# Two feed-forward networks behind attention: a second network's first products are threaded into a states' block, and late splits, stores and loads move by a few places

## The chip, the cores and the metric

The kernel runs on one core of a Trainium2 chip. The metric is the device time of one execution in microseconds; the time of a version is the median of its runs. TensorE (PE) does the matrix products, VectorE (DVE), ScalarE (ACT) and GpSimd (POOL) the work on their results, and SyncE (SP) issues nearly all DMAs of the stretch that is discussed here.

## The reference

Attention between 512 tokens and 32 states for 8 batches and 8 heads, then a gated network on all 8 x 544 rows of 512 columns, then a second network on the result:

```python
x = concatenate([softmax(x st') st, softmax(st x') x])   # per batch and head, D = 64
x = x.transpose(0, 2, 1, 3).reshape(B * S, H * D)         # 4352 rows, 512 columns
g = x @ w_gate                                            # 512 x 1536
x = (silu(g) * (x @ w_val)) @ w_out                       # first network
h = x @ w_in                                              # 512 x 2048
out = (maximum(h, 0) + alpha * minimum(h, 0)) @ w_out2    # second network
```

All is fp32. The kernel gets this precision from split operands: a number is the sum of a high part (`hi`, a copy rounded by ACT) and a low part (`lo`, the difference, made by DVE in `sub_lo`, L83), and a product is three matrix passes, high x high, high x low and low x high (`PASSES`). In the profile, ACT's line 77 is a copy (a high part or a move out of PSUM), and DVE's line 83 a low part.

## The kernel before

The work runs in stages. Attention and the first network of the 8 batches of 512 tokens come first, interleaved. Then comes the first network for the 256 state rows, the **states' block**: an object of class `Block` with n = 256 columns. Then the second network.

**The states' block.** `ffn1` goes through f = 0 to 11, the 128-wide blocks of the hidden layer: `gate(f)` (12 matmuls into bank g, then ACT's silu), `value(f)` (12 into bank v, then DVE's product, L488), `split(f)` (ACT's high and DVE's low part), and `project(f - 1)` (12 into four accumulators acc0 to acc3). Between these calls `fill(f, i)` runs what the table `slots` holds for the place: `split_w` (splitting later weights: ACT, then DVE), `x2_pair(0)` (the inputs of the second network's first pair of batches: loads, differences, high and low parts), `ahead` (weight loads). `finish` adds the last projection, copies the accumulators out and stores them (L512).

**The second network** takes the batches in pairs. A pair with a block of the hidden layer of 2 x 128 rows is a **step**, t = 0 to 31; steps 32 to 39 (`LAST` = 32, `hidden_last`) do the states. A step forms its 2 x 2 blocks of hidden values in 7 products, not 8, and has 7 **places**. Place by place `hidden_pair` makes one product of 6 matmuls (banks g, v, aux, v, g, v, aux) and what follows it on the other engines, and then `fill()` pops one item of the list `work`: half of a **link**, that is, one of the 14 half-steps (`link`, `project`, 6 matmuls, L1006) that put the hidden values of the two steps before through the output weights. A link's result is added to a running sum by DVE (L1017), or, the first time, copied by ACT (L77, sum<-acc). So in t = 2 to 31 TensorE alternates between a product and a link half.

The hidden values of a step are h00, h10, h11, h01 (`raised`: the leaky step, three ACT instructions L872 to L874 and one POOL addition L875); POOL then makes the four differences T1, T3, T2, T4 in this order (`less`, L915). All have to be split into high and low parts before the links use them; these splits fall into the next step, as the entries of the dictionary `left`, and `late(key)` runs them at written places: T1 at place 3, T3 at place 4, T2 and T4 at place 5.

**Other traffic.** `load_wo` (L993) loads a link's weights, three links ahead; at the end of an odd step the first three are loaded together, six DMAs. `load_w2` (L759) loads product weights. `give` (L1041 to L1044) turns a finished sum around with a DVE transpose and stores it with four DMAs, at every third place. `x2_sums` (L791, L792) makes differences of the next pair's inputs on DVE and stores them for a later load; `give_last` and `turn` do the last pair's output by transposes on TensorE.

**Order.** TensorE runs in written order throughout. In the loop over t = 0 to 31, DVE, ACT and POOL run in written order too (`manual_schedule`); SP, and all engines' work but TensorE's in the states' block and in t = 32 to 39, are put in order by the framework's scheduler. Every engine runs its own queue strictly in order: an instruction that waits holds all behind it.

Of the kernel before, what the change touches and what calls it, by code (L numbers as in the profile page):

```python
# [25 lines left out]
def attention_and_two_ffns(ctx: ExitStack, tc: tile.TileContext, x, state, w_gate, w_val,  # L26
                           w_out1, w_in2, w_out2, alpha, out):
    nc = tc.nc
# [430 lines left out]
    class Block:  # L459


        def __init__(self, n, lhs, rhs, nk, keep=False):
            self.n, self.lhs, self.rhs, self.nk, self.keep = n, lhs, rhs, nk, keep
            self.acc, self.p, self.hid = None, {}, {}

# [11 lines left out]
        def gate(self, f):  # L477

            if self.keep:
                if f % 2 == 0:  # L480
                    self.kept = t4([P, 2, S], F32, "p")
                self.p[f] = self.kept[:, f % 2]
            else:
                self.p[f] = t2([P, S], F32, "s")[:, :self.n]
            return nc.scalar.activation(self.p[f], self.product(f, 0, "g"), AF.Silu)

        def value(self, f):
            return nc.vector.tensor_tensor(out=self.p[f], in0=self.p[f], in1=self.product(f, 1, "v"),  # L488
                                           op=ALU.mult)
# [24 lines left out]
    def ffn1(blk, slots, before):  # L514
# [19 lines left out]
    with tc.manual_schedule(engines={mybir.EngineType.PE}):  # L534
# [248 lines left out]
        def x2_sums(pr):  # L783
# [108 lines left out]

        def hidden_pair(t, fill):
# [30 lines left out]
            def late(key):  # L924
                left.pop(key, lambda: None)()

# [5 lines left out]
            fill()  # L932
            v = psum([P, S], "v")
# [3 lines left out]
            fill()  # L937
            late("t1")
            y = aux([P, S])
            product(y, 2)  # L940
            fill()
            late("t3")
            product(v, 3, start=False)
# [8 lines left out]
            fill()  # L952
            product(v, 5, start=False)
# [4 lines left out]
            fill()  # L958
            product(y, 6, start=False)
# [3 lines left out]
            fill()  # L963
            lo("h00", h00)
# [10 lines left out]
            for k, o in (("t1", h00), ("t3", h01), ("t2", h11), ("t4", h10)):  # L975
                left[k] = lambda k=k, o=o: (hi(k, o), lo(k, o))

        acc, sums, put_in, giving, turning = {}, {}, set(), [], []
# [45 lines left out]
        def give(pr, to, e):  # L1024
# [17 lines left out]
            for i in range(4):  # L1042
                dst = out[c * T:c * T + S, d * P + 32 * i:d * P + 32 * i + 32]
                nc.sync.dma_start(dst.rearrange("(t r) n -> r t n", r=32), o[32 * i:32 * i + 32])  # L1044

        def give_last(pr, to, e):
# [6 lines left out]
            def turn():  # L1053
# [5 lines left out]
                nc.sync.dma_start(out[c * T:c * T + S, d * P:(d + 1) * P].rearrange("(k p) n -> p k n", k=SC), o)  # L1059
# [18 lines left out]
        def hidden_last(t, fill):  # L1078
            pr, s = STEPS[t]
            x, w = x2[pr], ws2.pop(t)  # L1080
            for f in range(2):
# [9 lines left out]
                h = hid["s", 2 * s + f] = t4([P, 2, S], F32R, "h2")  # L1091
                acopy(h[:, 0, :NS], m)
                sub_lo(h[:, 1, :NS], m, h[:, 0, :NS])
                fill()

# [7 lines left out]
        slots = {}  # L1103
        for f in range(2, NF1):
            slots.setdefault((f - 2, 0), []).append(lambda f=f: split_w(f))
        early = x2_pair(0)
        for i, th in enumerate(early):
            slots.setdefault((1 + i * (NF1 - 2) // len(early), 2), []).append(th)
        slots.setdefault((NF1 - 2, 2), []).append(lambda: [ahead() for _ in range(3)])

        def lhs(f, k, a, which):
            return ws[f][:, k, a, which, :]

        blk = Block(NS, lhs, lambda k, c: xs[0][:, k, c], NPAIR)
        ffn1(blk, slots, lambda: blocks[B - 1].finish(B - 1))
        blk.finish(B)

        LAST = (B // 2) * NJ2
        def step(t, pr, s):
            for n in ((t + 1,) if t == LAST - 1 else (t + 1, t + 2) if t == LAST else (t + 2,) if t > LAST else ()):  # L1120
                if n < len(STEPS):
                    load_last(n)
# [7 lines left out]
            def fill():  # L1130
                places[0] += 1
                for _ in range(len(turning)):
                    turning.pop(0)()
# [11 lines left out]
            (hidden_pair if t < LAST else hidden_last)(t, fill)  # L1145
# [11 lines left out]

        forming, work = {}, [lambda: None for _ in range(2 * 7 + 1)]
# [5 lines left out]
        for t in range(LAST, len(STEPS)):  # L1164
            step(t, *STEPS[t])
        for th in turning + work:
            th()
# [30 lines left out]
```

## Time and profile before

| what | value |
|---|---|
| time before, median of 3 runs | 1483.83 us (1479.69 to 1485.51) |
| profiled execution, its own time | 1478.91 us |
| span of the profiled execution, first to last instruction | 1477.1 us |
| mean granted TensorE clock | 0.981 of full speed |
| busy: PE | 1379.3 us, 93% |
| busy: DVE, ACT, POOL | 1033.7 us (70%), 822.6 us (56%), 558.8 us (38%) |

The table is read from the top: the runs give the time; the profile is one execution, and its own time is what durations read from the trace add up to. TensorE's busy share includes time at a lower granted clock, in which a matmul takes longer.

### The profile page before, as it was taken

To read this page: it belongs to the slowest core of one execution; us is meant where nothing else is said; L and a number is where in the kernel's file an instruction comes from. 1 tells how busy PE (TensorE), PEld (TensorE's weight loads), DVE (VectorE), ACT (ScalarE), POOL (GpSimd) and SP (SyncE) were. 2 spreads that over 40 slices of the span, in tenths; PEclk is the share of its full clock that TensorE was granted. 3 is DMA by queue.
4 is the path that set the end of the run, shared out by engine and by line. 5 is a ranking of instruction groups with operands and counts; after the bars stand their busy time and mean duration, and the time that the engine had idled before them with its cause. 6 is when DMAs were issued, how large, how long until landed. Compare 5 with 4: busy or idle time off the path is not lost.

```text
span 1477.1 us, 20530 instructions
## 1 busy us (share of the span) xinstructions
PE 1379.3 (93%) x7192; PEld 1067.1 (72%) x7192; DVE 1033.7 (70%) x1591; ACT 822.6 (56%) x1408; POOL 558.8 (38%) x422
## 2 busy tenths in 40 slices
PE   5799999999898999999989999999989999999897
PEld 2467776767676776778967777778777777778686
DVE  6778536678697877443756878778886788778740
ACT  6656344555655645333557566755656567655532
POOL 4432112233142322000046566545664565555611
PEclk7999999999999999999999999999999999999999
DMA  9442250676959575202264786779756987676772
GB/s 265 169 151 50 72 137 9 184 222 186 253 170 274 145 217 137 73 1 73 79 235 150 253 274 202 188 225 314 240 153 178 314 294 230 170 241 205 285 254 91
DMA packets 274224, 271.92 MB, mean 184 GB/s; under 512 B 133704, under 2 KB 198216, under 8 KB 273096
## 3 DMA queue, kind: packets, MB, share of 16 engines
q1 hardware_dynamic: 271976, 270.21, 59.1%
q8 instruction: 57, 0.93, 0.3%
q10 hardware_dynamic: 2144, 0.39, 0.2%
q14 instruction: 47, 0.39, 0.1%
HBM read 206.05 MB, written 64.49 MB: 183 GB/s over the span
## 4 chain that ended last, share of the span: by engine, by line
PE 57%; DVE 16%; ACT 10%; issue 6%; DMA 5%; POOL 4%; SPq 2%; POOLq 0%; ACTq 0%; DVEq 0%
PE acc L503 16%; PE v L472 9%; PE g L472 9%; PE acc L1006 8%; DVE h L83 6%; PE v L903 3%; PE aux L442 3%; DVE u L911 3%; PE g L903 2%; PE aux L903 2%; DMA wo<-ws2d 2%; ACT h L77 2%; DVE sum L1017 2%; ACT m L874 2%; DMA raw<-in_moe_w_out_dram 2%
## 5 line engine op out<-in xcount | busy, mean ns | idle before, releaser
L1006 PE MATMUL acc<-h,wo 128*128 128x512 f32 x1344 | 349.4, 396 | 36.5 <-DVE sum L1017 19.0
L1006 PEld LDWEIGHTS acc<-h,wo 128*128 128x128 f32 x1344 | 251.5, 190 | 101.2 <-DVE sum L1017 28.1
L503 PE MATMUL acc<-h,wp 128*128 128x512 f32 (+1 forms) x1296 | 297.1, 380 | 7.1 <-DVE h L83 3.7
L503 PEld LDWEIGHTS acc<-h,wp 128*128 128x128 f32 x1296 | 234.3, 189 | 57.7 <-DVE h L83 4.9
L875 POOL TENSOR_TENSOR u<-u,m 128x512 f32<-128x512 f32 x96 | 128.5, 1338 | 354.3 <-ACT m L874 322.7
L83 DVE TENSOR_TENSOR h<-u,h 128x512 fp32r<-128x512 f32 x160 | 159.0, 1009 | 69.4 <-ACT h L77 68.4
L472 PE MATMUL g<-a,sw 128*128 128x512 f32 x576 | 155.9, 405 | 9.7 <-ACT sw L77 5.4
L472 PEld LDWEIGHTS g<-a,sw 128*128 128x128 f32 x576 | 105.1, 190 | 71.3 <-issue 26.0
L472 PE MATMUL v<-a,sw 128*128 128x512 f32 x576 | 154.8, 405 | 0.1
L903 PE MATMUL v<-x,w 128*128 128x512 f32 x576 | 148.7, 394 | 5.0 <-DVE u L911 5.0
L872 ACT ACTIVATE m<-u 128x512 f32<-128x512 f32 x96 | 60.3, 628 | 157.8 <-DVE u L911 153.1
L1017 DVE TENSOR_TENSOR sum<-acc,sum 128x512 f32<-128x512 f32 x184 | 125.2, 681 | 27.2 <-PE acc L1006 26.9
L472 PEld LDWEIGHTS v<-a,sw 128*128 128x128 f32 x576 | 107.7, 192 | 33.8 <-issue 9.8
L903 PEld LDWEIGHTS v<-x,w 128*128 128x128 f32 x576 | 109.0, 190 | 30.0 <-DVE u L911 7.1
L83 DVE TENSOR_TENSOR h<-h,h 128x512 fp32r<-128x512 f32 (+1 forms) x80 | 77.7, 972 | 62.5 <-ACT h L77 62.0
L284 POOL TENSOR_TENSOR m<-m,raw 128x512 int32<-128x512 int32 x44 | 61.1, 1393 | 154.1 <-DVE m L276 75.2
L77 ACT ACTIVATE h<-u 128x512 fp32r<-128x512 f32 x160 | 96.6, 622 | 28.3 <-POOL u L915 28.3
L488 DVE TENSOR_TENSOR s<-s,v 128x512 f32<-128x512 f32 (+1 forms) x84 | 54.2, 645 | 81.8 <-PE v L472 68.3
L915 POOL TENSOR_TENSOR u<-u,u 128x512 f32<-128x512 f32 x64 | 103.1, 1611 | 5.0
L83 DVE TENSOR_TENSOR sw<-aux,sw 128x512 fp32r<-128x512 f32 x96 | 62.7, 683 | 56.3 <-ACT sw L77 56.3
L903 PE MATMUL aux<-x,w 128*128 128x512 f32 x384 | 101.1, 400 | 0.0
L77 ACT ACTIVATE h<-s 128x512 fp32r<-128x512 f32 (+1 forms) x84 | 50.3, 598 | 89.9 <-DVE s L488 89.7
(148 smaller groups left out, 2145.8 us busy)
## 6 DMA issues: line engine op xcount, KB each, us to landing
wo<-ws2d SPq DMA_DIRECT2D x224, 256.0 KB, 4.8
w<-w2d SPq DMA_DIRECT2D x104, 512.0 KB, 5.5
w2d<-sp SPq DMA_DIRECT2D x32, 512.0 KB, 4.0
raw<-in_moe_w_out_dram SPq DMA_DIRECT2D x14, 1024.0 KB, 5.0
x2r<-x2d SPq DMA_DIRECT2D x25, 512.0 KB, 5.8
w<-w2d SPq DMA_DIRECT2D x48, 256.0 KB, 5.1
x2d<-xo SPq DMA_DIRECT2D x32, 256.0 KB, 3.5
raw<-in_moe_w_in_dram SPq DMA_DIRECT2D x8, 1024.0 KB, 6.2
```

The lines of the kernel that those rows point to most:

```text
L77: return nc.scalar.activation(o, i, AF.Copy)
L83: (eng or nc.vector).tensor_tensor(out=o, in0=src, in1=hi.bitcast(F32), op=ALU.subtract)
L284: nc.gpsimd.tensor_tensor(out=m, in0=m, in1=lo, op=ALU.add)
L472: nc.tensor.matmul(o[:, :self.n], self.lhs(f, k, a, which), self.rhs(k, c), start=(i == 0), stop=(i == last))
L488: return nc.vector.tensor_tensor(out=self.p[f], in0=self.p[f], in1=self.product(f, 1, "v"), op=ALU.mult)
L503: nc.tensor.matmul(self.acc[e][:, :self.n], wo1[f // 2][:, f % 2, a, e * P:(e + 1) * P], t[:, c, :self.n], start=(f == 0 and i == 0), stop ...
L872: nc.scalar.activation(n, src, AF.Relu, scale=-1.0)
L875: nc.gpsimd.tensor_tensor(out=out, in0=out, in1=n, op=ALU.add)
L903: nc.tensor.matmul(o, w[:, a, q], x[k][:, q, e], start=start and n == 0, stop=stop and n == 5, skip_group_check=True)
L915: nc.gpsimd.tensor_tensor(out=o, in0=x0, in1=x1, op=ALU.subtract)
L1006: nc.tensor.matmul(o, w[:, f, a, e], h[:, q], start=first and i == 0, stop=i == 5, skip_group_check=True)
L1017: nc.vector.tensor_tensor(out=r, in0=o, in1=r, op=ALU.add)
```

## The change

Four things, in the order of the program:

1. **The states' block.** Its `split(f - 1)` is called behind `gate(f)` and not `split(f)` behind `value(f)`. Its four accumulators share two PSUM banks, as halves of acc0 and acc1; since two groups of matmuls then accumulate in one bank, both banks are set to zero by DVE (two 128x512 MEMSETs) ahead of `project(0)` and no matmul carries the start flag. From f = 7 on (`FROM`) the block's gate and value products go to acc2 and acc3, which frees g and v, and two products of steps t = 0 and 1 are called per f (10 of the 14 ahead of `finish`, 4 behind it). `x2_pair` is packed into f = 1 to 6, two items per f; before, it was spread over f = 1 to 10. To be called in parts, `hidden_pair` yields behind each place.
2. **T2 and T4.** Their high parts (ACT) are called at place 4, ahead of `raised(h11)`; their low parts (DVE) stay at place 5.
3. **Stores.** The four DMAs of `give` are issued two places later, the store of `x2_sums` three, that of `turn` one (the list `sending`).
4. **Order and the end.** SP is in written order now, and so are all engines in the states' block and in t = 32 to 39. In t = 32 and 33 the splits that step 31 left are run at places (`LATE`); before, all were run ahead of t = 32. The splits of `hidden_last` run one place later (`soon`), and `load_last` is called a little later.

```diff
@@ class Block
         def project(self, f):
             if f == 0:
-                self.acc = [psum([P, S], f"acc{e}") for e in range(NPAIR)]
+                if self.n == S:
+                    self.acc = [psum([P, S], f"acc{e}") for e in range(NPAIR)]
+                else:
+                    pairs = [psum([P, 2, self.n], f"acc{e}") for e in range(NPAIR // 2)]
+                    for t in pairs:
+                        nc.vector.memset(t, 0.0)
+                    self.acc = [pairs[e // 2][:, e % 2] for e in range(NPAIR)]
...
-                                     t[:, c, :self.n], start=(f == 0 and i == 0),
-                                     stop=(f == NF1 - 1 and i == 2))
+                                     t[:, c, :self.n], start=(self.n == S and f == 0 and i == 0),
+                                     stop=(f == NF1 - 1 and i == 2), skip_group_check=self.n < S)
...
             blk.gate(f)
+            if f and blk.n < S:
+                blk.split(f - 1)
             fill(f, 0)
             blk.value(f)
-            blk.split(f)
+            if blk.n == S:
+                blk.split(f)
@@ def x2_sums
-                nc.sync.dma_start(xt2d[pr - 1][:, k], r[to])
+                sending.append([3, lambda: nc.sync.dma_start(xt2d[pr - 1][:, k], r[to])])
@@ def hidden_pair
             late("t3")
+            late("t2 hi")
+            late("t4 hi")
             product(v, 3, start=False)
...
             fill()
-            late("t2")
-            late("t4")
+            yield
+            late("t2 lo")
+            late("t4 lo")
             product(g, 4, start=False)
@@ def give
-            for i in range(4):
...
-                nc.sync.dma_start(dst.rearrange("(t r) n -> r t n", r=32), o[32 * i:32 * i + 32])
+            def send():
...
+            sending.append([2, send])
@@ def step
+        LATE = {(0, 1): ("h10 hi", "h10 lo"), (0, 2): ("t1",), (1, 1): ("t3", "t2 hi", "t4 hi"),
+                (1, 2): ("t2 lo", "t4 lo")}
...
             def fill():
                 places[0] += 1
+                for e in list(sending):
+                    e[0] -= 1
+                    if not e[0]:
+                        sending.remove(e)
+                        e[1]()
...
+                for key in LATE.get((t - LAST, places[0]), ()):
+                    late(key)
+                for th in soon:
+                    th()
+                soon.clear()
@@ the states' block and the loop
-        with tc.manual_schedule(engines={mybir.EngineType.DVE, mybir.EngineType.Activation, mybir.EngineType.Pool}):
-            for t in range(LAST):
-                step(t, *STEPS[t])
-            for th in left.values():
-                th()
+        with tc.manual_schedule(engines={E.DVE, E.Activation, E.Pool, E.SP}):
...
+            for i, th in enumerate(x2_pair(0)):
+                slots.setdefault((1 + i // 2, 2), []).append(th)
+            slots.setdefault((4, 2), []).append(lambda: [ahead() for _ in range(3)])
+            first = (_ for t in range(2) for _ in step(t, *STEPS[t]))
+            for i in range(2 * (NF1 - FROM)):
+                slots.setdefault((FROM + i // 2, 0 if i % 2 == 0 else 2), []).append(lambda: next(first))
...
+            blk.banks = lambda f: ("g", "v") if f < FROM else ("acc2", "acc3")
+            ffn1(blk, slots, lambda: blocks[B - 1].finish(B - 1))
+            blk.split(NF1 - 1)
+            blk.finish(B)
+            for _ in first:
+                pass
```

How this moves instructions is shown at three places. First VectorE at the start of the states' block. The rows are those of f = 0 to 2: L488 (L489 in the changed file) is the product with bank v, `h` a low part of the block's hidden values, `ws` a low part of split weights. Before:

```order
L83 TENSOR_TENSOR h_1155_6319<-s_1151_6287,h_1155_6319 128x256
L80 COPY xo_1158_6340<-acc2_1086_5863 128x512
L488 TENSOR_TENSOR s_1160_6346<-s_1160_6346,v_1163_6364 128x256
L83 TENSOR_TENSOR h_1164_6378<-s_1160_6346,h_1164_6378 128x256
L488 TENSOR_TENSOR s_1174_6407<-s_1174_6407,v_1177_6425 128x256
```

and of the change:

```order
L83 TENSOR_TENSOR h_1161_6360<-s_1151_6289,h_1161_6360 128x256
L83 TENSOR_TENSOR ws_1162_6363<-wr_63_344,ws_1162_6363 128x4x256
L489 TENSOR_TENSOR s_1159_6345<-s_1159_6345,v_1163_6366 128x256
L505 MEMSET acc0_1164_6380 128x512
L505 MEMSET acc1_1165_6381 128x512
L848 TENSOR_TENSOR x2t_1170_6404<-x2r_1167_6398,x2r_1166_6396 128x1024
```

The two MEMSETs stand behind the low part of some weights and behind the second product with bank v. Next ScalarE at places 4 and 5 of step t = 5. `h<-u` and `h<-h` on L77 are high parts, L872 to L874 (L882 to L884 in the changed file) the leaky step of h11 and then of h00. Before:

```order
L77 ACTIVATE h2_1364_7606<-h_1360_7583 128x512
L77 ACTIVATE h2_1382_7717<-u_1369_7633 128x512
L872 ACTIVATE m_1385_7730<-u_1384_7728 128x512
L873 ACTIVATE u_1384_7728<-u_1384_7728 128x512
L874 ACTIVATE m_1385_7730<-m_1385_7730,alpha_sb_82 128x512
L77 ACTIVATE h2_1382_7717<-u_1356_7552 128x512
L77 ACTIVATE h2_1388_7747<-u_1363_7604 128x512
L872 ACTIVATE m_1391_7759<-g_1373_7651 128x512
```

and of the change:

```order
L77 ACTIVATE h2_1362_7605<-h_1358_7582 128x512
L77 ACTIVATE h2_1380_7715<-u_1367_7632 128x512
L77 ACTIVATE h2_1380_7715<-u_1354_7554 128x512
L77 ACTIVATE h2_1381_7719<-u_1361_7603 128x512
L882 ACTIVATE m_1384_7731<-u_1383_7729 128x512
L883 ACTIVATE u_1383_7729<-u_1383_7729 128x512
L884 ACTIVATE m_1384_7731<-m_1384_7731,alpha_sb_82 128x512
L882 ACTIVATE m_1389_7758<-g_1371_7651 128x512
```

The last two high parts of the differences, T2 and T4, stand ahead of the three instructions for h11 now. Last SP around the six loads at the end of step t = 11, the first weights of a new pair of steps' links (`wo2`). `out` x4 is a store of `give`, `w2` product weights, `x2r` inputs of a later pair. Before:

```order
L1044 DMA out_0_dram<-o_1587_8856 32x16x32 x4
L759 DMA w2_1589_8873<-w2d4_104 128x1024
L759 DMA w2_1595_8917<-w2d4_104 128x1024
L1044 DMA out_0_dram<-o_1601_8938 32x16x32 x4
L993 DMA wo2_1602_8945<-ws2d2_110 128x512
L993 DMA wo2_1602_8945<-ws2d3_111 128x512
L993 DMA wo2_1603_8948<-ws2d2_110 128x512
L993 DMA wo2_1603_8948<-ws2d3_111 128x512
L993 DMA wo2_1604_8951<-ws2d2_110 128x512
L993 DMA wo2_1604_8951<-ws2d3_111 128x512
L759 DMA w2_1606_8961<-w2d4_104 128x512
L780 DMA x2r_1608_8973<-x2d4_91 128x1024
```

and of the change:

```order
L1068 DMA out_0_dram<-o_1586_8859 32x16x32 x4
L769 DMA w2_1593_8917<-w2d4_104 128x1024
L1015 DMA wo2_1600_8941<-ws2d2_110 128x512
L1015 DMA wo2_1600_8941<-ws2d3_111 128x512
L1015 DMA wo2_1601_8944<-ws2d2_110 128x512
L1015 DMA wo2_1601_8944<-ws2d3_111 128x512
L1015 DMA wo2_1602_8947<-ws2d2_110 128x512
L1015 DMA wo2_1602_8947<-ws2d3_111 128x512
L769 DMA w2_1604_8957<-w2d4_104 128x512
L790 DMA x2r_1606_8969<-x2d4_91 128x1024
L790 DMA x2r_1607_8971<-x2d5_92 128x1024
L1068 DMA out_0_dram<-o_1599_8938 32x16x32 x4
```

The store that stood just ahead of the six loads stands three rows behind them; the store of the sum before it stands one row ahead of them.

## Rows read from the trace of the kernel before

**Rows 1.** Busy time by stretch (us): PE, PEld, DVE, ACT, POOL; granted clock; DMA share.

```profile
742.30:775.10 32.80, 26.36 (x105) 19.92 (x104) 17.81 (x20) 20.67 (x37) 15.26 (x12) 0.95 0.74 264
775.10:1388.10 613.00, 582.05 (x2497) 470.43 (x2496) 487.00 (x604) 383.92 (x662) 353.19 (x239) 0.99 0.71 226
...
981.00:983.00 2.00, 2.00 (x6) 1.58 (x5) 0.99 (x2) 0.00 (x0) 1.48 (x2) 0.52 1.03 352
```

**Rows 2.** TensorE in order of time: start, duration, instruction [idle before <-releaser].

```profile
696.06 1.60 PE L503 MATMUL acc<-h,wp 128*128 128x256 f32 x12
...
775.10 1.54 PE L903 MATMUL aux<-x,w 128*128 128x512 f32 x6
...
801.04 1.52 PE L903 MATMUL g<-x,w 128*128 128x512 f32 x6
...
803.76 1.52 PE L903 MATMUL v<-x,w 128*128 128x512 f32 x6
...
847.10 1.66 PE L1006 MATMUL acc<-h,wo 128*128 128x512 f32 x6 [1.03 <-DVE sum L1017]
...
979.73 2.24 PE L1006 MATMUL acc<-h,wo 128*128 128x512 f32 x6 [2.72 <-DMA wo<-ws2d]
...
1388.11 1.11 PE L1087 MATMUL g<-x,w 128*128 128x256 f32 x8
...
1401.37 2.93 PE L1006 MATMUL acc<-h,wo 128*128 128x512 f32 x6 [6.10 <-DVE sum L1017]
```

**Rows 3.** What TensorE waited for, 775.1 to 1388.1: total us, times, longest.

```profile
PE acc L1006 <- DVE sum L1017: 12.9, 18, 1.7
PE acc L1006 <- DMA wo<-ws2d: 11.6, 5, 3.8
PE acc L1006 <- ACT sum L77: 4.7, 3, 2.7
PE v L903 <- DVE u L911: 1.5, 3, 0.5
```

**Rows 4.** VectorE in order of time, places 4 and 5 of step t = 5.

```profile
844.47 1.98 DVE L83 TENSOR_TENSOR h<-u,h 128x512 fp32r<-128x512 f32 x2 [1.90 <-ACT h L77]
846.37 0.68 DVE L1017 TENSOR_TENSOR sum<-acc,sum 128x512 f32<-128x512 f32 x1
```

**Rows 5.** ScalarE in order of time: states' block, step t = 5, step t = 10.

```profile
694.82 0.38 ACT L485 ACTIVATE s<-g 128x256 f32<-128x256 f32 x1 [0.83 <-PE g L472]
696.79 0.42 ACT L77 ACTIVATE h<-s 128x256 fp32r<-128x256 f32 x1 [1.58 <-DVE s L488]
...
842.01 0.63 ACT L872 ACTIVATE m<-u 128x512 f32<-128x512 f32 x1 [5.17 <-DVE u L911]
...
843.82 1.14 ACT L77 ACTIVATE h<-u 128x512 fp32r<-128x512 f32 x2
...
943.91 0.63 ACT L872 ACTIVATE m<-u 128x512 f32<-128x512 f32 x1 [3.01 <-DVE u L911]
```

**Rows 6.** GpSimd in order of time, the differences T4 of three steps.

```profile
837.95 2.15 POOL L915 TENSOR_TENSOR u<-u,u 128x512 f32<-128x512 f32 x1
...
942.02 1.63 POOL L915 TENSOR_TENSOR u<-u,u 128x512 f32<-128x512 f32 x1
...
1397.73 1.27 POOL L915 TENSOR_TENSOR u<-u,u 128x512 f32<-128x512 f32 x1
```

**Rows 7.** SP's DMA queue in order of time, end of step t = 11.

```profile
974.71 1.97 SPq L1044 DMA_DIRECT2D out_dram<-o  x4
976.78 2.83 SPq L993 DMA_DIRECT2D wo<-ws2d  x6
```

**Rows 8.** Groups by line: count, ns min/median/max, first and last start.

```profile
L83 DVE TENSOR_TENSOR ws<-wr,ws x9: 1217/1219/1227, 686.2 to 722.4; 128x1024 fp32r<-128x1024 f32 x9
L77 ACT ACTIVATE ws<-wr x8: 1042/1046/1061, 687.5 to 719.3; 128x1024 fp32r<-128x1024 f32 x8
...
L93 DVE MEMSET bd<- x2: 272/272/272, 0.9 to 1.2; 128x256 f32 x2
```

More of the change, by code (lines that the diff above doesn't have):

```diff
@@ L464, in __init__ @@
             self.acc, self.p, self.hid = None, {}, {}
+            self.banks = lambda f: ("g", "v")
         def product(self, f, which, tag):
@@ L484, in gate @@
                 self.p[f] = t2([P, S], F32, "s")[:, :self.n]
-            return nc.scalar.activation(self.p[f], self.product(f, 0, "g"), AF.Silu)
+            return nc.scalar.activation(self.p[f], self.product(f, 0, self.banks(f)[0]), AF.Silu)
         def value(self, f):
-            return nc.vector.tensor_tensor(out=self.p[f], in0=self.p[f], in1=self.product(f, 1, "v"),
+            return nc.vector.tensor_tensor(out=self.p[f], in0=self.p[f], in1=self.product(f, 1, self.banks(f)[1]),
                                            op=ALU.mult)
@@ L891, in attention_and_two_ffns, with late @@
         left = {}
+        def late(key):
+            left.pop(key, lambda: None)()
         def hidden_pair(t, fill):
@@ L974, in hidden_pair @@
             left["h10 lo"] = rest
-            for k, o in (("t1", h00), ("t3", h01), ("t2", h11), ("t4", h10)):
+            for k, o in (("t1", h00), ("t3", h01)):
                 left[k] = lambda k=k, o=o: (hi(k, o), lo(k, o))
-        acc, sums, put_in, giving, turning = {}, {}, set(), [], []
+            for k, o in (("t2", h11), ("t4", h10)):
+                left[k + " hi"] = lambda k=k, o=o: hi(k, o)
+                left[k + " lo"] = lambda k=k, o=o: lo(k, o)
+        acc, sums, put_in, giving, turning, sending, soon = {}, {}, set(), [], [], [], []
         def store(u, o):
@@ L1041, in give @@
             nc.vector.transpose(out=o.rearrange("p t n -> p (t n)"), in_=y)
-            for i in range(4):
-                dst = out[c * T:c * T + S, d * P + 32 * i:d * P + 32 * i + 32]
-                nc.sync.dma_start(dst.rearrange("(t r) n -> r t n", r=32), o[32 * i:32 * i + 32])
+            def send():
+                for i in range(4):
+                    dst = out[c * T:c * T + S, d * P + 32 * i:d * P + 32 * i + 32]
+                    nc.sync.dma_start(dst.rearrange("(t r) n -> r t n", r=32), o[32 * i:32 * i + 32])
+            sending.append([2, send])
         def give_last(pr, to, e):
@@ L1058, in turn @@
                 acopy(o, pt)
-                nc.sync.dma_start(out[c * T:c * T + S, d * P:(d + 1) * P].rearrange("(k p) n -> p k n", k=SC), o)
+                sending.append([1, lambda: nc.sync.dma_start(
+                    out[c * T:c * T + S, d * P:(d + 1) * P].rearrange("(k p) n -> p k n", k=SC), o)])
             turning.append(turn)
@@ L1101, in ahead @@
                 coming.pop(0)()
[L1103 to L1116, printed above, removed]
         LAST = (B // 2) * NJ2
+        LATE = {(0, 1): ("h10 hi", "h10 lo"), (0, 2): ("t1",), (1, 1): ("t3", "t2 hi", "t4 hi"),
+                (1, 2): ("t2 lo", "t4 lo")}
         def step(t, pr, s):
-            for n in ((t + 1,) if t == LAST - 1 else (t + 1, t + 2) if t == LAST else (t + 2,) if t > LAST else ()):
-                if n < len(STEPS):
-                    load_last(n)
+            if t == LAST:
+                load_last(t + 1)
             if s == 1 and pr + 1 < B // 2:
@@ L1131, in fill @@
                 places[0] += 1
+                for e in list(sending):
[3 more added lines that the diff above has]
+                        e[1]()
+                if t == LAST - 1 and places[0] == 4:
+                    load_last(LAST)
+                if t >= LAST and places[0] == 1 and t + 2 < len(STEPS):
+                    load_last(t + 2)
+                for key in LATE.get((t - LAST, places[0]), ()):
[3 more added lines that the diff above has]
+                soon.clear()
                 for _ in range(len(turning)):
@@ L1144, in step @@
                 x2_last()
-            (hidden_pair if t < LAST else hidden_last)(t, fill)
+            if t < LAST:
+                yield from hidden_pair(t, fill)
+            else:
+                hidden_last(t, fill)
             if t >= LAST:
```

35 lines of the change are left out of this document (27 added, 8 removed).

## The prediction

> **What bounds the kernel now.** I read busy time by stretch first, then TensorE in order of time. From step t = 2 to the end of step 31, 613 us, TensorE is busy 582.05 us and no other engine over 487.00 us [rows 1]: TensorE sets the pace, and its losses are what can be won. An undisturbed place is a product and a link half in 803.76 - 801.04 = 2.72 us [rows 2]. From the product at 775.10 to the first of step 32 at 1388.11 there are 5 places of step 2 and 7 in each of steps 3 to 31: 208 x 2.72 = 565.8 us of the 613.0. So **47.2 us are lost**. TensorE's waits in this stretch sum to 12.9 + 11.6 + 4.7 + 1.5 = 30.7 us [rows 3]. The rest is slow running after them: behind the 2.72 us wait at 979.73 the granted clock is 0.52 of full speed for two microseconds, that is, the lower of its two levels (1.2 GHz) for nearly all of that time [rows 1, 2]. A microsecond of wait thus costs 47.2 / 30.7 = 1.54 us. Two more losses lie outside. From 742.30 to 775.10 TensorE runs 17 groups of 6 matmuls (steps 0 and 1, and three groups of step 2), 17 x 1.36 = 23.1 us of work in 32.8: 9.7 lost [rows 1]. And it waits 6.10 us at 1401.37 in step 32 [rows 2].
>
> **Part 2, T2 and T4: the sums' waits.** At place 5 VectorE waits 1.90 us for ScalarE, makes two low parts in 1.98 us and only then the link's sum, at 846.37 [rows 4]; TensorE's next link half needs the bank that this sum empties and starts at 847.10, 1.03 us late [rows 2]. ScalarE makes these two high parts at 843.82, behind the three instructions for h11, for which it stood idle 5.17 us [rows 5]. GpSimd had T4 ready at 837.95 + 2.15 = 840.10 [rows 6]. With the high parts in front of h11's instructions they can run from 840.10 to 841.24, which is 0.77 us before those could start at 842.01. VectorE, idle from 844.47 - 1.90 = 842.57, then finds them done, and the next sum is some 1.90 us earlier: more than the 1.03 us of the wait. The edit adds no instruction. Its cover is that idle time, and it is thinner elsewhere: in step 10 T4 is ready at 943.65 and h11 starts at 943.91 [rows 6, 5], so one high part of 0.57 us makes h11 0.3 us late, on ScalarE, which has idle time behind it.
> All waits for sums, 12.9 + 4.7 = 17.6 us [rows 3], come within some 6 us behind such a pair of low parts. VectorE is busy 487 of 613 us, and will be 487 of about 577, 84%, so some will come back where several low parts and a difference of the next inputs fall on one place. I take three quarters, 13 us; ends: half, 9, and all, 17.6. The 1.5 us for u stay.
>
> **Part 3, the stores: the waits for weights.** SP waits until a transposed sum is ready, issues its four DMAs in 1.97 us from 974.71, and only then the six loads of the next links' weights, from 976.78 [rows 7]; TensorE's link has been waiting for them since 977.01 and starts at 979.73 [rows 2]. Now this store stands behind the six loads, and the one ahead of them is two places old, so its data are ready. The loads go at least the 1.97 us earlier, and SP's wait before it goes too. Five such waits make 11.6 us [rows 3]; five times 1.97 is 9.9. I take 10.6; ends: 8 (a store ahead still costs something) and 11.6.
> A rule of the Trainium skill speaks against this (DMA: Bandwidth & Descriptors, section "Issuing engines are not separate DMA queues"): all DMAs end up on the same 16 engines, and the time to issue one is usually small beside the transfer. By it the move would win little, and the sum below would lose its 10.6. Here the issue of one store alone is 1.97 us of a wait of 2.72 us, so I go by the row; the rule's outcome is a rival below.
> Parts 2 and 3 together: (13 + 10.6) x 1.54 = **-36.3 us**; ends (9 + 8) x 1.54 = -26.2 and (17.6 + 11.6) x 1.54 = -45.0.
>
> **Part 1, the states' block.** The gain: 10 of the 14 products of steps 0 and 1 stand between products of the block and so have their waits covered. At most the 9.7 us. The cost: until now the block has TensorE gapless. `project(0)` would be due at 696.06 [rows 2]. It now waits for a MEMSET of its bank, and that one stands on VectorE behind the second value product, behind a low part of weights, behind ScalarE's high part of them, behind the high part of the hidden values, behind the second silu. In durations: the silu ends at 694.82 + 0.38 = 695.20 [rows 5]; high part 0.42 [rows 5]; ws high 1.05 and ws low 1.22 [rows 8]; value product 0.42, taken as long as that high part of the same width; a MEMSET of 128x512, of which the trace has none: twice the 0.27 of a 128x256 one [rows 8] is 0.54, at least 0.27. Sum: 698.85, so TensorE waits **2.8 us**, and 1 to 1.8 more at the lower clock behind it, by the 1.54. When I lay out the changed order with such durations, four later f lose 0.2 to 0.4 us and f = 5 about 1.5, since `split(f - 1)` gives each low part less lead and `x2_pair`'s differences, packed into six f, stand ahead of it. That makes 6 to 7 us. The four products left behind `finish` and the first link halves keep about 3 us of the old waits. Net: -9.7 + 6.5 + 3 = **0**; ends -6 (VectorE and ScalarE in a better order than I lay out) and +7 (also the second half of the block stalls).
>
> **Part 4, the end.** At 1401.37 TensorE waits for sums that stand on VectorE behind the left-over splits, the last of which needs T4 from GpSimd at 1397.73 [rows 2, 6]. Spread over two steps, the sums no longer stand behind them. The splits of `hidden_last` one place later cost one short wait of about 1 us at the first half of a states' product, by laying the rows out. -6.1 + 1 and the slow clock behind: **-5.5**; ends -3 and -7. The last steps' chain is as before. `load_last` later and stores of the last pair one place later cost nothing as long as SP's loads come a whole step (some 5 us) ahead of their use.
>
> **Sum.** -36.3 + 0 - 5.5 = -42 on the profiled execution's 1478.9, so 1437. The runs before lie 0.8 to 6.6 us above that execution, their median 4.9; I add 4: **1441 us**. With all ends: 1478.9 + 4 - 45.0 - 6 - 7 = 1425, and 1478.9 + 4 - 26.2 + 7 - 3 = 1461.
>
> **Rivals.**
> - *VectorE takes the place of the wait.* The waits move to other sums, since VectorE at 84% has no room, and of part 2 only a quarter is won, 4 us: (4 + 10.6) x 1.54 + 5.5 = 28 won: about 1455; with nothing won, 1461. For it: low parts of 0.99 us x 2 stand ahead of every such sum still. Against: VectorE's idle 1.90 us lies before the pair, so the pair moves as a whole. The Trainium skill has a rule that points this way (Perfetto Trace Analysis, section "Optimization Strategy"): a bubble that repeats on the engine that should be full can mean too few buffers for the next tile, here accumulator banks, which the change doesn't add.
> - *The weights come late anyway*, because the transfers themselves are late: part 3 wins 2 us of 11.6. (13 + 2) x 1.54 + 5.5 = 28.6 won, about 1454. Against it: five waits alone, each behind a store.
> - *The states' block stalls through*: at f = 7 to 11 bank and low part come late each time, 2 us at each of 5 f and the lower clock, +15: 1456.
> - *Slower: GpSimd's T4 is late at place 4.* Then ScalarE's queue holds h11's three instructions behind the wait, and h11, h00 and all that follow are late in each step. The rows show 0.77 us and -0.3 us of room. To undo 42 us and 7 more over 30 steps it takes 1.6 us on TensorE in each. Against it: GpSimd is busy 353 of 613 us [rows 1] and starts these differences from the step before, and shorter waits of TensorE between there and place 4 are only the five for weights. The time then: 1490.
>
> **Chances.** My forecast 0.62; VectorE 0.11, weights 0.06, states' block 0.06 (all three faster still); all waits gone and the transition's too (1425 or less) 0.03; T4 late 0.12, of which 0.07 at the 1.2 to 1.6 us a step that cancel the gains and 0.05 beyond. The range 1425 to 1462 takes in the first four. Under 0.5%, 7.4 us, a measurement can't tell a change from none. Faster by more than that: 0.88; within: 0.07; slower: 0.05.
>
> **What would show it.** Right: TensorE's waits between step 2 and 32 down from 30.7 to about 8 us; none for wo over 1 us; no wait of VectorE for ScalarE ahead of the two low parts; a wait of about 3 us of `project(0)` for a MEMSET; a wait under 1.5 us in step 32. Wrong: ScalarE waiting for GpSimd ahead of h11's instructions (L882); SP's loads of wo waiting for a transposed sum; TensorE waiting for sums as long as before.

## The result, and the profile after

The changed kernel takes 1432.38 us (median of 4 runs, 1428.03 to 1433.43) against 1484.67 us for the kernel before (median of 4): ratio 0.9643, 95% interval 0.9604 to 0.9681. The forecast was 1441 us, with a range of 1425 to 1462. The profiled execution takes 1428.03 us, 50.9 us less than that of before.

Where the 50.9 us come from is read from three marks on TensorE: the first product of the states' block, the product of step 2 at place 3, and the first product of step 32. The start of the states' block alone lies between 686.8 and 694.5 us in the kernels below, whose work ahead of it is the same, so whole times hide small differences that the first two stretches show: kernels with the same instructions in them agree within 0.1 us from the block to step 2 (changed, stores back, splits flushed) and within 0.5 us in steps 2 to 31 (changed, old states' block, splits flushed and the three with early MEMSETs). The last stretch is less exact: with the same instructions it takes 83.7 or 85.3 us, and 1.5 us of that are its last twelve matmuls (3.41 us in the changed kernel, 4.87 with early MEMSETs). The kernels ran in several batches, in which the kernel before took 1482.3 to 1484.7 us; each ratio is taken within its batch.

| kernel | block to step 2 | steps 2 to 31 | step 32 to the end | median of all runs |
|---|---|---|---|---|
| before | 87.5 | 613.0 | 89.0 | 1484.7 |
| changed | 87.3 | 568.4 | 83.7 | 1432.4 |
| T2 and T4 alone | 86.7 | 581.1 | 89.5 | 1451.2 |
| stores alone | 87.5 | 600.4 | 91.6 | 1470.5 |
| changed, high parts back | 88.5 | 597.6 | 84.3 | 1465.3 |
| changed, stores back | 87.3 | 608.0 | 85.4 | 1471.3 |
| changed, old states' block | 86.8 | 568.6 | 83.6 | 1432.0 |
| changed, splits flushed | 87.3 | 568.7 | 90.4 | 1436.9 |
| changed, early MEMSETs | 88.9 | 568.9 | 85.3 | 1433.0 |
| early MEMSETs and loads | 84.4 | 568.5 | 83.7 | 1430.7 |
| these, items one f later | 84.3 | 568.8 | 85.3 | 1428.3 |
| one more low part | 87.3 | 577.7 | 83.7 | 1439.5 |
| two more low parts | 87.7 | 606.8 | 83.5 | 1474.8 |
| same dose elsewhere | 88.1 | 587.8 | 84.1 | 1454.4 |

So steps 2 to 31 give 44.6 us (forecast 36.3), the end 5.3 (5.5), the states' block and what follows it 0.25 (0); the other 0.8 us lie ahead of the first mark. Steps 2 to 31 by engine, with the columns of [rows 1]:

```profile
774.08:1342.51 568.43, 566.88 (x2497) 468.03 (x2496) 481.34 (x604) 390.48 (x663) 350.95 (x240) 1.00 0.77 250
```

TensorE is busy 566.9 of 568.4 us at a granted clock of 1.00, the higher of its two levels (2.4 GHz); 208 undisturbed places are 565.8. Its waits from 774 to 1350, the counterpart of [rows 3]:

```profile
PE acc L1028 <- ACT sum L77: 1.3, 2, 0.9
PE acc L1028 <- DVE h L83: 0.9, 1, 0.9
PE acc L1028 <- DVE sum L1039: 0.3, 1, 0.3
```

The row for weights and that for u are gone, and the 18 waits for VectorE's sums are one. (The 0.9 us for a low part lie at 773.51, ahead of the mark.) How this comes about is seen at places 4 and 5 of step 5, first on ScalarE, then on VectorE, then on GpSimd; [rows 4, 5] have the same places of before:

```profile
836.59 0.63 ACT L77 ACTIVATE h<-u 128x512 fp32r<-128x512 f32 x1 [1.07 <-POOL u L928]
839.60 0.63 ACT L882 ACTIVATE m<-u 128x512 f32<-128x512 f32 x1 [2.38 <-DVE u L924]
```

```profile
839.48 0.68 DVE L1039 TENSOR_TENSOR sum<-acc,sum 128x512 f32<-128x512 f32 x1
840.08 1.28 DVE L83 TENSOR_TENSOR h<-u,h 128x512 fp32r<-128x512 f32 x2
841.28 0.68 DVE L1039 TENSOR_TENSOR sum<-acc,sum 128x512 f32<-128x512 f32 x1
```

```profile
841.59 1.30 POOL L885 TENSOR_TENSOR u<-u,m 128x512 f32<-128x512 f32 x1 [5.04 <-ACT m L884]
```

T4's high part runs as soon as GpSimd has T4, in time that ScalarE has to spare (2.38 us more follow). VectorE goes from sum to low parts to sum without a wait. And the pair takes 1.28 us, not 1.98. On VectorE this is so in every step: before, it stood idle ahead of 29 of the 30 pairs, 55.7 us in all, and now ahead of none. These are its waits for ScalarE ahead of the low parts of all hidden values, before and then of the change:

```profile
DVE h L83 <- ACT h L77: 82.3, 49, 3.7
...
DVE h L83 <- ACT h L77: 26.3, 25, 2.8
```

ScalarE doesn't have that room in every step. In step 10 h11 is ready at 935.52, but T4's high part still stands ahead of its first instruction:

```profile
935.39 0.63 ACT L77 ACTIVATE h<-u 128x512 fp32r<-128x512 f32 x1 [1.07 <-POOL u L928]
935.92 0.62 ACT L882 ACTIVATE m<-u 128x512 f32<-128x512 f32 x1
```

In all 30 steps ScalarE waits for GpSimd ahead of T4's high part, and in 17 of them h11 starts 0.2 to 0.4 us late by it. TensorE has no wait from it.

On SP's queue at the end of step 11 (of before: [rows 7]):

```profile
956.18 1.95 SPq L1068 DMA_DIRECT2D out_dram<-o  x4
...
958.77 3.08 SPq L1015 DMA_DIRECT2D wo<-ws2d  x6
...
964.52 2.63 SPq L1068 DMA_DIRECT2D out_dram<-o  x4
```

The last store stands behind the six loads. The store ahead of them still waits for its transposed sum: VectorE ends that transpose (the first row below) at 956.15, SP has waited 6.1 us for it, and the loads follow 2.6 us later. But this sum is the one before, three places earlier, so the loads are issued at 958.77 for a link that starts without a wait at 965.76, 7.0 us ahead of it; before, they were issued 0.2 us ahead of the time the link was due, 977.01 [rows 2, 7]. SP's waits for transposed sums in steps 2 to 31 shrink by a fifth only; the last two rows have them, before and of the change:

```profile
955.44 0.71 DVE L1063 STREAM_TRANSPOSE o<-y 128x512 f32<-128x512 f32 x1
...
965.76 1.52 PE L1028 MATMUL acc<-h,wo 128*128 128x512 f32 x6
...
SPq L1044 <- DVE o L1041: 111.6, 24, 8.6
...
SPq L1068 <- DVE o L1063: 89.6, 23, 7.7
```

On TensorE the wait for the MEMSET is there, the end has one short wait for a sum (in step 33, ahead of the transposes of a finished sum), and the marks stand on these rows:

```profile
698.08 1.66 PE L510 MATMUL acc<-h,wp 128*128 128x256 f32 x12 [2.62 <-DVE acc L505]
...
774.08 1.55 PE L916 MATMUL aux<-x,w 128*128 128x512 f32 x6
...
1342.51 1.60 PE L1114 MATMUL g<-x,w 128*128 128x256 f32 x12
...
1353.74 0.66 PE L1082 MATMUL aux<-ident,sum 128*128 128x128 f32 x4 [1.27 <-DVE sum L1039]
```

### The profile page after: what moved, and what is told of

Same layout as the page of the kernel before. It is cut to its first block, busy times and chain, and to the rows that moved or that the text cites. A ratio compares the mean times of both kernels' runs of the same rounds, so it can differ in the third digit from the quotient of the medians.

```text
span 1426.2 us, 20519 instructions
## 1 busy us (share of the span) xinstructions
PE 1361.8 (95%) x7192; PEld 1062.7 (75%) x7192; DVE 1032.1 (72%) x1593; ACT 825.6 (58%) x1408; POOL 555.0 (39%) x422
## 4 chain that ended last, share of the span: by engine, by line
PE 75%; DVE 7%; ACT 4%; DMA 4%; issue 4%; POOL 3%; SPq 1%; ACTq 0%; POOLq 0%; DVEq 0%
PE acc L1028 17%; PE acc L510 16%; PE v L473 9%; PE g L473 8%; PE v L916 7%; PE g L916 5%; PE aux L916 5%; PE aux L442 3%; DMA raw<-in_moe_w_out_dram 2%; DVE h L83 2%; PE acc L1098 1%; POOL u L928 1%; DMA wo<-ws2d 1%; POOL u L885 1%; DVE sw L83 1%
## 5 line engine op out<-in xcount | busy, mean ns | idle before, releaser
L1028 PE MATMUL acc<-h,wo 128*128 128x512 f32 x1344 | 341.4, 390 | 2.5 <-ACT sum L77 1.3
L83 DVE TENSOR_TENSOR h<-u,h 128x512 fp32r<-128x512 f32 x160 | 148.9, 947 | 23.7 <-ACT h L77 23.3
L77 ACT ACTIVATE h<-u 128x512 fp32r<-128x512 f32 x160 | 100.2, 630 | 88.2 <-POOL u L928 87.2
L489 DVE TENSOR_TENSOR s<-s,v 128x512 f32<-128x512 f32 (+1 forms) x79 | 52.0, 658 | 68.3 <-PE v L473 54.5
L884 ACT ACTIVATE m<-m,alpha_sb 128x512 f32<-128x512 f32 (+1 forms) x144 | 99.2, 689 | 0.0
L77 ACT ACTIVATE h<-s 128x512 fp32r<-128x512 f32 (+1 forms) x84 | 50.2, 598 | 83.5 <-DVE s L489 83.2
L916 PE MATMUL g<-x,w 128*128 128x512 f32 x384 | 97.6, 390 | 0.7 <-ACT h L883 0.7
```

Of the source, the lines that this page charges most:

```text
L77: return nc.scalar.activation(o, i, AF.Copy)
L83: (eng or nc.vector).tensor_tensor(out=o, in0=src, in1=hi.bitcast(F32), op=ALU.subtract)
L884: nc.scalar.activation(n, n, AF.Copy, scale=alpha_sb[:, f:f + 1])
L916: nc.tensor.matmul(o, w[:, a, q], x[k][:, q, e], start=start and n == 0, stop=stop and n == 5, skip_group_check=True)
L1028: nc.tensor.matmul(o, w[:, f, a, e], h[:, q], start=first and i == 0, stop=i == 5, skip_group_check=True)
```

## The experiments

**T2 and T4 alone**, put into the kernel before:

```diff
             late("t3")
+            late("t2 hi")
+            late("t4 hi")
             product(v, 3, start=False)
...
-            late("t2")
-            late("t4")
+            late("t2 lo")
+            late("t4 lo")
```

> The kernel before with part 2 alone: the high parts of T2 and T4 at place 4, all else as before. Theory (each edit takes its own waits away): TensorE's waits for sums between step 2 and 32 (17.6 us before) and for u (1.5) go, the waits for weights (11.6 us) stay; -19 us x 1.54 = -29, about 1455. Rival (the waits cover one another, or VectorE sets the pace): without the stores' move less than half of it, 1470 or more.

It takes 1451.24 us, ratio 0.9778 (0.9756 to 0.98), with 31.9 us off steps 2 to 31. TensorE's waits there, 30.7 us before, sum to 10.8:

```profile
PE acc L1011 <- DMA wo<-ws2d: 9.1, 3, 4.2
PE acc L1011 <- ACT sum L77: 1.2, 2, 0.9
PE acc L1011 <- DVE sum L1022: 0.5, 1, 0.5
```

The theory holds: the waits for sums go but for 1.7 us, those for u go, and those for weights stay. Three of the five are left; the largest of before, 3.75 us at 1106.43, went too, and why is not shown.

**The stores alone**, put into the kernel before, with SP in the scheduler's order (`sending` as in the change).

> The kernel before with the later stores alone (two and three places), SP still ordered by the scheduler, the high parts where they were. Theory: the five waits for weights, 11.6 us, go; -11.6 x 1.54 = -18, about 1466; waits for sums stay at 17 us. Rival (it is SP's written order that brings the weights earlier, not the later stores): no gain here, 1480 or more. Rival (the transfers themselves are late): the five waits stay, 1480 or more.

It takes 1470.53 us, ratio 0.9911 (0.9891 to 0.993), with 12.6 us off the stretch. Its waits (those for u stay at 1.5):

```profile
PE acc L1006 <- DVE sum L1017: 13.9, 19, 1.7
PE acc L1006 <- ACT sum L77: 5.7, 4, 2.8
PE acc L1006 <- DMA wo<-ws2d: 1.8, 2, 1.4
```

The waits for weights fall from 11.6 to 1.8 us, so the transfers are not late in themselves, and it doesn't take SP's written order: both rivals fall. The gain is smaller than the 18 us expected. The waits for sums grow from 17.6 to 19.6; probably VectorE had used part of the waits for weights to catch up, which is not shown. What the two edits win alone adds up to what the change wins: 31.9 + 12.6 = 44.5 against 44.6.

**The changed kernel with one of them taken back.** First the high parts:

```diff
-            late("t2 hi")
-            late("t4 hi")
...
+            late("t2 hi")
             late("t2 lo")
+            late("t4 hi")
             late("t4 lo")
```

> The changed kernel with the high parts of T2 and T4 back at place 5. Theory: the waits for sums come back, some 18 us, and with the clock 28 us: about 1460. Rival (in the changed order they would be covered anyway): under 1445.

It takes 1465.26 us, ratio 0.9874 (0.9852 to 0.9897), 29.2 us more in steps 2 to 31. Waits for sums are back (13.4 us in 19 waits, and 4.8 in 3 for ScalarE's), for weights hardly (1.0):

```profile
PE acc L1028 <- DVE sum L1039: 13.4, 19, 1.7
PE acc L1028 <- ACT sum L77: 4.8, 3, 2.7
...
PE acc L1028 <- DMA wo<-ws2d: 1.0, 2, 0.6
```

Then the stores, issued at once, with SP in written order:

```diff
-                sending.append([3, lambda: nc.sync.dma_start(xt2d[pr - 1][:, k], r[to])])
+                nc.sync.dma_start(xt2d[pr - 1][:, k], r[to])
...
-            sending.append([2, send])
+            send()
```

> The changed kernel with the stores of sums and of input differences issued at once again, SP still in written order. Theory (the place of the store in SP's queue counts): about 12 us of waits for weights come back, 1432 + 18 = 1450. Rival (written order of SP counts, not the delay): 1436 or less.

It takes 1471.27 us, ratio 0.9908 (0.9885 to 0.993): 39.6 us of the stretch are given back, twice what was expected. The waits for weights are not five and 11.6 us as before, but ten:

```profile
PE acc L1028 <- DMA wo<-ws2d: 27.0, 10, 5.8
```

This is one of them, first on SP's queue and then on TensorE:

```profile
932.38 1.94 SPq L1068 DMA_DIRECT2D out_dram<-o  x4
934.42 0.45 SPq L769 DMA_DIRECT2D w<-w2d  x1
934.97 2.86 SPq L1015 DMA_DIRECT2D wo<-ws2d  x6
```

```profile
939.37 2.93 PE L1028 MATMUL acc<-h,wo 128*128 128x512 f32 x6 [5.23 <-DMA wo<-ws2d]
```

VectorE's transpose ends at 932.35, the store starts then, the six loads 2.6 us later, and the link, due at 934.14, starts at 939.37. Written order without later stores is thus worse than the scheduler's order, with which the high parts alone had 581.1 us in this stretch against 608.0 here. The theory on the store's place holds, but its price was too low by half. Three of the ten waits, 6.4 us, stand behind stores of input differences (L802), and none of the five before did; for part of the price the scheduler's order had thus kept such stores out of the loads' way.

**The old states' block in the changed kernel** (the block ahead of the loop, by the scheduler; all of part 1 taken back).

> The changed kernel with the states' block as before (its own stage, ordered by the scheduler, steps 0 and 1 behind it), all else as changed. Theory (what the threading covers, the block loses again at its MEMSET and its late low parts): no difference over 3 us, 1430 to 1436. Rival (the threading is worth its 8 to 9 us): 1440 or more.

It takes 1432.0 us, ratio 0.9655 (0.9633 to 0.9677): no difference, as the theory has it. From the block to step 2 it takes 86.8 us against 87.3. It has the waits that the threading covers, two of them for u in steps 0 and 1 with 5.1 us, and none in the block; the changed kernel has the 2.62 us for the MEMSET and later ones for low parts.

**The splits of step 31 flushed ahead of step 32** in the changed kernel:

```diff
             if t == LAST:
+                for key in list(left):
+                    late(key)
                 load_last(t + 1)
```

> The changed kernel with the splits that step 31 leaves run all at once ahead of step 32, as before. Theory: TensorE waits for sums in step 32 again, 4 to 6 us, 1437. Rival (the wait came from the scheduler's order in that stage): under 1434.

It takes 1436.93 us, ratio 0.9686 (0.9664 to 0.9707). The end takes 6.7 us longer, of which 1.6 are the last twelve matmuls (5.00 us against 3.41), whose time differs among kernels with the same end too; and the wait for sums is back:

```profile
PE acc L1028 <- DVE sum L1039: 5.3, 2, 4.7
```

**The MEMSETs earlier**, at f = 0 right behind the copies that empty the banks; the new method `clear` holds what `project` did for them at f = 0:

```diff
...
-            ffn1(blk, slots, lambda: blocks[B - 1].finish(B - 1))
+            ffn1(blk, slots, lambda: (blocks[B - 1].finish(B - 1), blk.clear()))
```

> The changed kernel with the two MEMSETs of the states' block right behind the copies that empty these banks, at f = 0, and not ahead of the first projection. Theory: the wait of 2.62 us at the first projection goes and nothing takes its place: 2.6 to 4 us faster, 1428 to 1430. Rival (the projection waits for its low part next, which stands behind the same split of weights): under 1 us faster.

It takes 1432.96 us, ratio 0.9662 (0.9637 to 0.9688): nothing is won, as in the rival, though not at the place it named, and from the block to step 2 it takes 1.6 us more than the changed kernel. The first projection starts on time, and the second waits. VectorE, then TensorE:

```profile
708.92 1.22 DVE L849 TENSOR_TENSOR x2t<-x2r,x2r 128x1024 f32<-128x1024 f32 x1 [4.06 <-DMA x2r<-x2d]
710.06 0.42 DVE L83 TENSOR_TENSOR h<-s,h 128x256 fp32r<-128x256 f32 x1
```

```profile
707.13 0.28 PE L511 MATMUL acc<-h,wp 128*128 128x256 f32 x1
710.53 2.02 PE L511 MATMUL acc<-h,wp 128*128 128x256 f32 x11 [3.13 <-DVE h L83]
```

VectorE is held by the first difference of the next stage's inputs, whose loads (issued behind stores at f = 1) have not landed, and the block's low part stands behind it. In the changed kernel VectorE waits for these loads too, 2.64 us at 701.11, but there TensorE is late already by its wait for the MEMSET and has no wait at the second projection. So the loads were issued at f = 0, and in a second kernel all later items moved back by one f as well:

```diff
-                slots.setdefault((1 + i // 2, 2), []).append(th)
+                slots.setdefault((1 + i // 2, 2) if i else (0, 0), []).append(th)
```

> The early MEMSETs, and the four loads of the second network's first inputs issued at f = 0 instead of f = 1, ahead of the stores. Theory (VectorE stood 4 us waiting for these loads with a low part of the block behind it): the 3.13 us wait goes as well, and now the MEMSETs' 2.6 us are won: 1426 to 1430. Rival (the loads come no earlier, being held by buffers): as early_memset, 1433.

> As the early MEMSETs and loads, and all items of the first pair's inputs behind the loads one f later (f = 2 to 7 instead of 1 to 6). Theory: if the loads still come too late for the difference at f = 1, this one has no wait in the block: 1426 to 1429; if not, the same as the run without the shift. Rival (the items then crowd the threaded part from f = 7 on): 1432 or more.

They take 1430.66 us, ratio 0.9626 (0.9603 to 0.9649), and 1428.28 us, ratio 0.963 (0.9606 to 0.9654). From the block to step 2 they take 84.4 and 84.3 us, 2.9 and 3.0 less than the changed kernel; no wait of the block is over 0.7 us. So the early loads make the early MEMSETs pay, and the shift by one f adds nothing. The whole times can't tell this from the changed kernel (the intervals overlap), the stretch can.

**VectorE's room.** Low parts were made twice, with the same values: T2's and T4's at place 5 (two more), T4's alone (one more), or h11's at place 6 and h00's at the end of place 7 (same dose elsewhere).

```diff
-                left[k + " lo"] = lambda k=k, o=o: lo(k, o)
+                left[k + " lo"] = lambda k=k, o=o: [lo(k, o) for _ in range(2)]
```

> The changed kernel with the two low parts at place 5 (T2, T4) made twice, the same values again: two more VectorE instructions in each step, 1.2 to 2 us. Theory (VectorE has room: it waits for others over 2 us a step): TensorE's waits grow by under 6 us in all, 1434 to 1440. Rival (VectorE is just short of the bound, and every microsecond more at place 5 delays a sum): 30 steps of about 1.2 us and the clock, 1470.

> The changed kernel with two other low parts made twice, the same values again: that of h11 at place 6 and that of h00 at the end of place 7, so VectorE has the dose of the run with two more low parts, but not at place 5. Theory (VectorE as a whole has no room left, so the dose counts and not its place): 1465 to 1480, as there. Rival (place 5, where the pair stands ahead of a sum, is the crowded place): under 1450.

> The changed kernel with one low part at place 5 (T4's) made twice, the same values again: half the dose of the run with two. Theory (VectorE has some idle time at that place, and only what goes beyond it delays a sum): clearly under half of the 38 us that two cost in steps 2 to 31, 3 to 12 us there, 1436 to 1445. Rival (VectorE has no idle time left there, each microsecond counts from the first on): 19 us, 1451.

In the order of these three expectations, the kernels take 1474.82 us (ratio 0.9937, 0.9915 to 0.996), 1454.35 (0.9793, 0.9771 to 0.9815) and 1439.51 (0.9715, 0.969 to 0.974). In steps 2 to 31 two more cost 38.3 us, the same dose elsewhere 19.4, one more 9.2. Steps 2 to 31 by engine for two more, the same dose elsewhere and one more, with the columns of [rows 1], and then what TensorE waited for with two more:

```profile
777.57:1384.33 606.76, 577.85 (x2497) 466.56 (x2496) 551.71 (x664) 390.06 (x661) 369.65 (x239) 1.00 0.74 234
...
775.89:1363.71 587.82, 574.36 (x2498) 467.64 (x2496) 530.36 (x663) 391.45 (x662) 356.38 (x240) 1.00 0.76 241
...
774.95:1352.62 577.67, 571.31 (x2497) 466.94 (x2496) 511.49 (x634) 391.71 (x663) 362.45 (x240) 1.00 0.77 246
```

```profile
PE acc L1028 <- DVE sum L1039: 21.5, 17, 2.8
PE v L916 <- DVE u L924: 4.1, 6, 0.9
```

The theory for two more fell: VectorE has no 2 us a step to give. That on one more holds: it costs a quarter of what two cost. On the place neither theory does: the same 60 instructions cost half as much at places 6 and 7. But in time they aren't the same dose. VectorE is busy 481.3 us in the changed kernel, 511.5 with one more, 530.4 with the dose elsewhere and 551.7 with two more, so 30.2, 49.0 and 70.4 us were added, and they cost 9.2, 19.4 and 38.3 us. That is one rising curve, steeper the more is added; whether the place counts beyond the time that an instruction takes there is not shown.

## Why the prediction was right

**The waits for sums: right in mechanism, the term of 13 us too small.** The forecast was that three quarters of 17.6 us go, that some come back with VectorE at 84%, and that the 1.5 us for u stay. All but 1.6 us went, and the 1.5 us for u too; part 2 alone won 31.9 us, where 13 x 1.54 = 20.0 were set. VectorE is busy 481 of 568 us, 85%, as worked out, and yet nothing came back: it lost its own waits for ScalarE ahead of these low parts, as said, 55.7 us in 30 steps. That this room is thin is shown by the doses: the rival that VectorE sets the pace was false here, and would be true with one or two more instructions per step.

**The waits for weights: right in that the store's place counts, too dear, and with one premise wrong.** In the changed kernel all 11.6 us are gone. Done alone, the move took away 9.8 (10.6 forecast), but 2.0 came back as waits for sums, and it won 12.6 us, where 10.6 x 1.54 = 16.3 were set. So the sum of both parts, 36.3 against 44.6, is 12 us too low in one term and 4 too high in the other. The premise that the store left ahead of the loads has its data ready didn't come true: SP still waits for a transposed sum there, 6.1 us at 956.18, which the forecast had named as a sign of being wrong. It does no harm because that sum is the one before, and the loads come 7.0 us ahead of their use. The Trainium skill's rule (DMA: Bandwidth & Descriptors, "Issuing engines are not separate DMA queues") is that DMAs of all issuing engines run on the same 16 DMA engines. As the prediction applied it, the move would win little. In the run with the stores back it is worth 39.6 us, because SP runs its queue strictly in order and a store that waits for VectorE holds the loads. The Trainium skill's rule on repeated gaps (Perfetto Trace Analysis, "Optimization Strategy") is that they can mean too few buffers. Here they didn't: the repeated gap went without one more buffer.

**1.54 us for a microsecond of wait: right as a mean, its cause only in part.** Lost time by waits in the same stretch is 47.2 / 30.7 before, (581.1 - 565.8) / 10.8 = 1.42 for T2 and T4 alone and (608.0 - 565.8) / 27.7 = 1.52 with the stores back. But the forecast put all 16.5 us beyond the waits down to slow running. Read in stretches of 2 us, the granted clock before falls clearly below full speed at four places only, behind waits of 2.7 to 3.8 us; an estimate from these stretches is 6.8 us in all. Behind the 18 waits for VectorE's sums, none over 1.7 us, it doesn't fall, nor behind the wait for weights of 2.31 us at 1149.96. The rest is mostly the edge of a wait: undisturbed, groups of six matmuls start every 1.36 us and last 1.52, so 0.16 us of overlap is lost ahead of a wait, and the group behind it lasts 0.14 longer, 1.66 us at 847.10 [rows 2]. By an estimate from these rows, 29 waits cost 29 x 0.30 = 8.7 us in this way. By this estimate many short waits cost more than their sum even at the full clock.

**The states' block: right, 0, in part by luck.** A wait of 2.62 us for the MEMSET stands where 2.8 were worked out, and the stretch is 0.25 us shorter. That the whole of part 1 is worth nothing is shown by taking it back. Reckoned from the starts of TensorE's rows (twelve matmuls of 256 columns take 1.44 us there undisturbed, six of 512 take 1.36), the block loses 6.9 us (6.5 forecast) and 2.6 stay behind it (3). Inside the 6.9 two terms are off and cancel: behind the MEMSET's wait there is no slow running (the granted clock is 1.00 from 698 to 704 us; 1 to 1.8 us were set), f = 5 loses 1.4 (1.5), and the other f lose 2.7, about twice what was laid out. What the forecast didn't see is the wait for loads behind the one for the MEMSET.

**The end: right.** It is 5.3 us against 5.5, though this stretch is exact to 1.6 us only; the flushed run puts it down to the splits. A wait of 1.27 us is there where about 1 was expected, but not at a states' product: it is ahead of the transposes of a finished sum. At the states' products two waits of 2.2 us for ScalarE's high parts stand where one of 1.8 us stood before.

**T4 late from GpSimd: it came true, but too small to count.** ScalarE waits for GpSimd ahead of T4's high part in every step, 1.07 us at 836.59, which the forecast had named as a sign of being wrong too. In 17 of 30 steps h11 is late by it, as in step 10 by 0.40 us, where 0.3 were worked out. TensorE's waits show nothing of it; the rival needed 1.6 us a step on TensorE.

## What to carry to other kernels

Taking away the wait of an instruction whose releaser could have run earlier can be worth more than the wait, because of what is queued behind it; look at the idle time of the engine it waits for. On a queue that runs in order, as SP's here, a store that waits for its data belongs behind the loads that are needed soon, the more so if the order is written by hand. Before a wait is taken out, look for the next one behind it in the same queue, and before work is put on an engine with idle time, try it with a dose: here, at 85% busy, 1.0 us more in a step of 19 cost 0.3 us, and 2.3 us more cost 1.3. And when an instruction's place is judged by how much time it adds, read that time in the new place.

## What the hardware showed unexpectedly

VectorE's low part of 128x512 takes 0.64 us or up to 1.8 us. At place 5 the pair took 1.97 or 1.98 us in 20 of 30 steps before, with GpSimd's addition beside it, as at 844.47 [rows 4], and 1.29 us in the six steps where GpSimd was idle, as at 864.00. GpSimd's row at the first of these, then VectorE's and GpSimd's at the second:

```profile
844.00 1.30 POOL L875 TENSOR_TENSOR u<-u,m 128x512 f32<-128x512 f32 x1 [3.90 <-ACT m L874]
...
864.00 1.29 DVE L83 TENSOR_TENSOR h<-u,h 128x512 fp32r<-128x512 f32 x2 [2.85 <-ACT h L77]
...
866.14 2.03 POOL L875 TENSOR_TENSOR h<-h,m 128x512 f32<-128x512 f32 x1 [2.27 <-ACT m L874]
```

In the changed kernel the pair takes 1.25 to 1.30 us in 26 of 30 steps, mostly in time in which GpSimd idles, as the 5.04 us above. In five of these steps GpSimd's addition starts during the pair; then the pair keeps its 1.28 us and the addition takes longer, as the 1.73 us at 899.11. The sums, which read one operand from PSUM, keep to 669 to 692 ns throughout:

```profile
L1017 DVE TENSOR_TENSOR sum<-acc,sum x168: 669/678/692, 798.5 to 1386.9; 128x512 f32<-128x512 f32 x168
```

The Trainium skill has this (SBUF — State Buffer, "Who interferes with whom"): a VectorE instruction with two inputs in SBUF contends with a GpSimd instruction that reads SBUF, and one with at most one input there doesn't, outside the 2-port modes. The rows agree. So moving the pair earlier also made most pairs shorter, by 0.7 us each, which the forecast hadn't counted. But four pairs got longer (2.36 to 3.46 us), so that all 30 take 43.9 us, 9.2 less than before, and since other instructions got longer too, VectorE's busy time falls from 487.0 to 481.3 us only. How much of the 44.6 us that is was not measured by itself.
